# Threshold attention and an ELU feed-forward on one core: head pairs 5 to 9 take the two-step structure, and the first stage is ordered from a list of jobs with needs

## The chip, the cores and the metric

The kernel runs on one core of one Trainium2 chip. The metric is the device time of one execution in microseconds (us), and lower is better. The engines are named as the profile names them: PE (matrix products, with PEld for its weight loads), DVE (vector engine), ACT (activation engine), POOL (GpSimd) and SP, from whose queue nearly all transfers are issued. Each engine executes its own instructions in the order in which the program lists them; semaphores join the engines.

## The reference

There are 8 sequences of 576 tokens with 8 heads of 64 channels, all fp32. Attention keeps only the scores that lie within `tau` of the row's maximum; its output, 4608 tokens by 512 channels, goes through two matrix products with an ELU between them (512 to 2048 to 512).

```python
def _attn_ref(q, k, v, tau):
    scale = 1.0 / np.sqrt(q.shape[-1])
    scores = scale * np.matmul(q, k.transpose(0, 1, 3, 2))
    thresh = np.max(scores, axis=-1, keepdims=True) - tau
    scores = np.where(scores >= thresh, scores, -1000000000.0)
    scores = scores - np.max(scores, axis=-1, keepdims=True)
    attn = np.exp(scores)
    attn = attn / (np.sum(attn, axis=-1, keepdims=True) + 1e-09)
    return np.matmul(attn, v).astype(np.float32)

def _moe_ref(x, w_in, w_out):
    h = x @ w_in
    g = np.where(h > 0.0, h, np.exp(np.minimum(h, 0.0)) - 1.0)
    return (g @ w_out).astype(np.float32)
```

## The kernel before

**Pairs and steps.** Two heads form a pair, four pairs a sequence, so there are 32 pairs, numbered 0 to 31 in the code (pairs 5 to 9 of the title are 4 to 8 there, and the code's numbers are used from here on). A pair has five steps: four row blocks of 128 query tokens (both heads, 576 scores per row and head) and one step for the last 64 tokens of both heads together (`NC`). A step goes through these operations: scores on PE (`scores`), the row maximum on DVE (`max_of`), the bound on POOL (`bound_of`), the exponential on ACT (`exp_of`), the mask with its row sum on DVE (`mask_of`), the sum of the two head sums and a reciprocal on DVE (`total_of`, `reciprocal_of`), and the normalization on POOL (`normalize`). Then the weights must be transposed. Either PE does it in three or two parts through a PSUM bank and ACT copies the result (`turn_parts`), or DVE turns 32x32 squares and four stores to DRAM and one load put the squares in place (`turn_squares`, `fetch`). Last come the products with `v` (`values`, `values_out`).

**The two-step structure.** Pairs 9 to 31 run in a loop at the end of the kernel that holds one set of five PSUM banks (`wide`) for all scores. A pair has a short tail step, in which its 64-token scores share PE with the values of the pair before the last (`tails_and_values`), and two halves, each of which writes the scores of two row blocks and two heads at once into the five banks (`wide_scores`). The next writing of a bank waits for the masks that read it. The weights live in just two buffers (`turned_by`), and all steps are turned in squares. After each half, 14 quarters of the feed-forward (`first_product`, `second_round`, a Strassen-like scheme with seven products in place of eight, 0.86 us each) are put on PE. The loop's order comes from `on_pe`, `at` and a table of written shifts, `MOVED`.

**The first stage.** Everything ahead of that loop is made by `early_tasks`: all of pairs 0 to 8 in the one-step structure (score buffers of two banks per head, three weight buffers), the first sequence's feed-forward in 64 plain halves (`ffn1`, `ffn2_plain`, 8 or 4 products each), the conversion of the 32 pieces of `w_in` and `w_out` from their raw words (`convert_rest`, `convert_shift`, `convert_add`, `convert_abs`, `convert_end` on ACT, DVE, POOL, ACT and DVE), and the sums of weight blocks that the loop's scheme needs (`make_in`, `change_in`, `make_out`). `task` gives each of these a written time, from a base of 5.0 us a step for ten steps and 7.2 us a step after that, shifted by `MOVED`; the program is listed in the order of these times, each task's needs ahead of it. In the first ten steps `spare` puts transposes of the identity on PE, 132 with those at the start. At the change from the first stage's pools to the loop's, `leave_early` closes one pool and opens another in its place.

**What decides the order of other queues.** SP's queue takes loads, stores of turned squares and fetches in the same listing; an entry that waits for a semaphore holds up what is behind it.

## Time and profile before

| | us |
|---|---|
| three runs, median (lowest to highest) | 1306.32 (1305.8 to 1308.91) |
| span of the profiled execution, first to last instruction | 1304.1 |
| span to median of the runs | 2.2 |
| first stage: start to the first tail step of pair 9 | 284.7 |
| of that, DVE busy | 231.1 |
| one pair of the loop, from pair 11's tail step to pair 12's | 34.1 |

The page of the profile has a row of busy tenths for each engine in 40 slices of 32.6 us, and the trace can be asked for busy times of stretches, for groups of equal instructions, for waits and for the instructions in order of time. PE matmuls are pipelined: their durations overlap, so what one costs is read from the distance between starts. A PE that counts as busy can still have gaps within a group.

### The profile page before, as it was taken

How to read it: one execution, taken by the hardware profiler on the slowest of the kernel's cores; microseconds unless marked ns; L12 is line 12 of the kernel's file. 1: busy time of each engine (PE TensorE's matmuls, PEld its weight loads, DVE VectorE, ACT ScalarE, POOL GpSimd, SP SyncE). 2: the span in 40 equal slices, each digit the busy share in tenths (PEclk: the TensorE clock that was granted, in tenths of full speed). 3: DMA queues.
4: the chain of work that ended last, by engine and by line, in shares of the span. 5: the costliest groups of instructions: out<-in, count | busy, mean ns of one | idle time of the engine just before them, and what ended most of it. 6: DMA issues, size and time to landing. Idle time of an engine off the chain costs nothing.

```text
span 1304.1 us, 21747 instructions
## 1 busy us (share of the span) xinstructions
PE 1278.2 (98%) x6822; PEld 994.8 (76%) x6822; DVE 1022.4 (78%) x2218; ACT 552.0 (42%) x1196; POOL 800.6 (61%) x1190
## 2 busy tenths in 40 slices
PE   9999999889999999999999999999999999999998
PEld 7675566346888887878878878878787888888887
DVE  6888887789888988898889889897989882545534
ACT  5777633225252535344444444353525260421320
POOL 4678645878466765766576747574858473524533
PEclk9999999899999999999999999999999999999999
DMA  7546377788888999899889888989899875222211
GB/s 148 125 149 175 99 208 201 224 212 259 216 242 238 260 229 254 224 253 232 226 221 263 236 238 219 257 242 246 221 260 252 228 217 171 85 73 68 86 61 33
DMA packets 327828, 256.02 MB, mean 196 GB/s; under 512 B 209312, under 2 KB 288672, under 8 KB 327712
## 3 DMA queue, kind: packets, MB, share of 16 engines
q1 hardware_dynamic: 325776, 254.14, 71.0%
q8 instruction: 54, 0.88, 0.3%
q10 hardware_dynamic: 1936, 0.48, 0.2%
q14 instruction: 62, 0.51, 0.1%
HBM read 165.94 MB, written 88.60 MB: 195 GB/s over the span
## 4 chain that ended last, share of the span: by engine, by line
PE 85%; DVE 5%; POOL 3%; issue 2%; DMA 1%; ACT 1%; SPq 1%; DVEq 0%; POOLq 0%; ACTq 0%
PE f L1441 30%; PE f L1301 28%; PE sc L663 7%; PE sc L723 7%; PE f L774 3%; PE sc L393 3%; PE rt L471 2%; PE f L814 2%; PE pv L616 1%; POOL w L427 1%; DVE w L454 1%; PE sc L715 1%; PE sc L710 1%; DVE mx L431 1%; DMA there<-x 1%
## 5 line engine op out<-in xcount | busy, mean ns | idle before, releaser
L427 POOL TENSOR_SCALAR w<-w,rs 128x576 f32<-128x576 f32 x196 | 163.1, 841 | 88.5 <-DVE rs L468 85.7
L670 DVE TENSOR_REDUCE mx<-sc 128x1 f32<-128x576 f32 x207 | 148.2, 749 | 29.7 <-PE sc L663 25.8
L680 ACT ACTIVATE w<-sc,mx 128x576 f32<-128x576 f32 x115 | 82.9, 740 | 118.3 <-DVE mx L670 96.4
L1301 PE MATMUL f<-xt,sw 128*128 128x256 f32 x512 | 124.2, 385 | 1.0 <-ACT xt L733 0.5
L1301 PE MATMUL f<-xt,w_in_sb 128*128 128x256 f32 x512 | 122.2, 381 | 0.1
L550 DVE STREAM_TRANSPOSE x<-w 128x512 f32<-128x512 f32 (+2 forms) x163 | 107.2, 692 | 13.9 <-POOL w L427 13.6
L676 POOL TENSOR_SCALAR th<-mx,ntau 128x2 f32<-128x2 f32 (+1 forms) x115 | 34.3, 299 | 136.1 <-DVE mx L670 136.1
L1301 PEld LDWEIGHTS f<-xt,sw 128*128 128x128 f32 x512 | 93.7, 190 | 21.3 <-issue 5.2
L1301 PEld LDWEIGHTS f<-xt,w_in_sb 128*128 128x128 f32 x512 | 96.2, 190 | 15.9 <-ACT w L1315 2.7
L1301 PE MATMUL f<-x,w_in_sb 128*128 128x256 f32 x448 | 106.1, 379 | 1.4 <-ACT g L1362 1.4
L1441 PE MATMUL f<-w_out_sb,g 128*128 128x256 f32 x448 | 107.1, 382 | 0.0
L1441 PE MATMUL f<-w_out_sb,s 128*128 128x256 f32 x448 | 107.0, 382 | 0.0
L1441 PE MATMUL f<-t,s 128*128 128x256 f32 x448 | 105.8, 379 | 0.0
L663 PE MATMUL sc<-kT,qT 64*128 64x448 f32 (+4 forms) x736 | 103.2, 416 | 1.4 <-DVE w L684 1.4
L663 PEld LDWEIGHTS sc<-kT,qT 64*128 64x128 f32 x736 | 80.6, 186 | 26.4 <-issue 16.8
L1388 POOL TENSOR_TENSOR s<-g 128x256 f32<-128x256 f32 x104 | 80.4, 778 | 29.4 <-PE f L1441 20.1
L684 DVE SCALAR_TENSOR_TENSOR w<-sc,th,w 128x576 f32<-128x576 f32 x115 | 89.7, 810 | 10.3 <-ACT w L680 10.1
L1301 PEld LDWEIGHTS f<-x,w_in_sb 128*128 128x128 f32 x448 | 85.0, 190 | 13.3 <-ACT g L1362 1.8
L1441 PEld LDWEIGHTS f<-w_out_sb,g 128*128 128x128 f32 x448 | 84.1, 190 | 14.2 <-issue 3.2
L1441 PEld LDWEIGHTS f<-w_out_sb,s 128*128 128x128 f32 x448 | 84.2, 190 | 13.5 <-issue 2.5
L1441 PEld LDWEIGHTS f<-t,s 128*128 128x128 f32 x448 | 85.1, 190 | 11.6
L427 POOL TENSOR_SCALAR e<-e,rs 128x576 f32<-128x576 f32 x92 | 68.5, 748 | 35.3 <-DVE rs L468 33.8
(204 smaller groups left out, 2813.1 us busy)
## 6 DMA issues: line engine op xcount, KB each, us to landing
there<-x SPq DMA_DIRECT2D x436, 144.0 KB, 3.4
wTb<-there SPq DMA_DIRECT2D x56, 576.0 KB, 6.5
wTa<-there SPq DMA_DIRECT2D x53, 576.0 KB, 4.9
sw<-win_sums SPq DMA_DIRECT2D x62, 384.0 KB, 4.2
t<-wout_sums SPq DMA_DIRECT2D x45, 512.0 KB, 5.5
qm<-in_q_dram SPq DMA_DIRECT2D x124, 72.0 KB, 4.7
vm<-in_v_dram SPq DMA_DIRECT2D x64, 128.0 KB, 3.1
wst<-in_moe_w_in_dram SPq DMA_DIRECT2D x16, 512.0 KB, 4.6
```

The costliest lines, as they stand in the source:

```text
L393: nc.tensor.matmul(scs[h][:, a, :HALF], qs[r], kT[r, k0 : k0 + HALF], start=True, stop=True)
L427: nc.gpsimd.tensor_scalar(wv, wv, st["rs"][:, h : h + 1], 1.0, ALU.mult, ALU.mult)
L550: nc.vector.transpose(x[:, :, c0 : c0 + nc_], src.rearrange("p (c g n) -> p g c n", c=nc_, n=T))
L663: on_banks(nc.tensor.matmul(o, qT[r, i * P : (i + 1) * P], kT[r, k0 : k0 + n], start=True, stop=True, skip_group_check=True), o)
L670: on_banks(nc.vector.tensor_reduce(st["mx"][:, h : h + 1], st["sc", h], axis=AX.XY if i == NC else AX.X, op=ALU.max, negate=True), st["sc" ...
L680: on_banks(nc.scalar.activation(st["e", h], st["sc", h], AF.Exp, bias=st["mx"][:, h : h + 1]), st["sc", h])
L684: on_banks(nc.vector.scalar_tensor_tensor(st["e", h], st["sc", h], st["th"][:, h : h + 1], st["e", h], ALU.is_ge, ALU.mult, accum_out=st[" ...
L723: on_banks(nc.tensor.matmul(o, vm[:, h, c], parts[part][:, g0:g1, h * (NC + 1) + c], start=False, stop=(c == NC - 1), skip_group_check=Tru ...
L774: nc.tensor.matmul(loc["ph"][:, k], w_in_sb[:, j, ft * P : (ft + 1) * P], xts[g][:, j, hf * CT : (hf + 1) * CT], start=(j == 0), stop=(j = ...
L1301: nc.tensor.matmul(loc["banks"][place], left[:, j], right[:, j], start=(begins and j == 0), stop=(j == 1), skip_group_check=True)
L1388: engine.tensor_tensor(o, x, y, op)
L1441: nc.tensor.matmul(place(m), lhs, rhs, start=(begins and v == 0), stop=(v == RU - 1), skip_group_check=True)
```

## The change

Pairs 4 to 8 leave the one-step structure: `JOINED` (the first pair in two steps) goes from 9 to 4, while the loop still starts with pair 9, now called `START`. The whole of the first stage is expressed as jobs: each has an engine, a written cost, a written due time, the jobs that it needs, and the PSUM banks that it uses. `schedule` keeps one clock per engine and repeatedly lists the job that can start first by those clocks; on an engine, jobs that can start within a small allowance of the earliest are taken by due time. The numbers of the due times stand in a table `PR` in place of most of `MOVED`; the entries of `MOVED` for the loop stay as they were.

With it come these edits:

- The five banks of `wide` exist from the start. Pairs 0 to 3 use four of them as two score buffers, the fifth and three further banks are lent out by `schedule` for transposes, values and feed-forward.
- The order of pairs 0 to 3 is all first row blocks, all second ones, then the rest pair by pair; the values of the first two row blocks are formed one block at a time (`values(..., block=...)`), and half of the first sequence's `ffn1` works on 128 tokens at a time (`ffn1_block`).
- One weight buffer and the two square buffers get pools that last for the whole kernel; two weight buffers serve pairs 4 to 8, as in the loop.
- 32 of the first stage's normalizations and 14 of its sums go to ACT (`normalize_act`, `total_act`), 10 `convert_rest` and 16 of 24 `make_in` go to POOL.
- Steps of pairs 4 to 8 are turned in squares except two of pair 4; of pairs 0 to 3 one step is turned in squares.
- Transposes of the identity are put on PE only in gaps before 24 us of the scheduler's clock (`PR["warm"]`), 127 in all.
- The values of pair 7 move into the tail step of pair 9, and the input sums of the second sequence (`sums_x`) into the loop's pair 9.

```diff
+PR = {'wait_pe': 0.262,
+ 'wait_dve': 0.141,
+ 'wait_act': 0.187,
...
+ 'b0': 6.944,
+ 'p0': 4.249,
+ 'p1': 6.0,
+ 'p2': 24.241,
...
+ 'warm': 24.083,
+ 'part_b': [[4, 0], [4, 2], [5, 1], [5, 2], [6, 3]],
+ 'squares': [12]}
...
+    def convert_rest_pool(i):
+        if i in staged:
+            lo = staged[i][:, :, 0]
+            nc.gpsimd.tensor_scalar(lo.bitcast(FP32), lo, 2.0**-51, 2.0, ALU.mult, ALU.add)
...
+    turned_by = w_one, e_both.rearrange("p e a n -> p (e a n)")
...
-        if "f" in psum and not apart:
-            both = psum["s"].tile([P, 2, 2, 512], FP32, name="sc")
-            scs = {h: both[:, h] for h in hs}
-        else:
-            scs = {h: psum["s"].tile([P, 2, 512], FP32, name="sc") for h in hs}
+        for h in hs:
+            scs[h] = slots[slot_no[0] % 2]
+            slot_no[0] += 1
...
+    def normalize_act(pr, i, h):
+        st = open_steps[pr, i]
+        wv = st["w"][:, h * S : (h + 1) * S]
+        nc.scalar.mul(wv, wv, st["rs"][:, h : h + 1])
+
+    def total_act(pr, i, hs):
+        st = open_steps[pr, i]
+        cs = slice(hs[0], hs[-1] + 1)
+        st["summed"] = True
+        nc.scalar.activation(st["su"][:, cs], st["sm"][:, cs, 0], AF.Identity, bias=st["sm"][:, 0, 1:2])
...
-            for _ in range(spare.pop() if spare else 0):
-                transpose(rt[:, 0], ident)
...
+    def ffn1_block(i, x):
+
+        loc = {}
+
+        def part(k):
+            if k == 0:
+                loc["ph"] = bank()
+            for a in range(2 * k, 2 * k + 2):
+                ft = 4 * x + a
+                for j in range(KJ):
+                    nc.tensor.matmul(loc["ph"][:, a * P : (a + 1) * P], w_in_sb[:, j, ft * P : (ft + 1) * P],
+                                     xts[0][:, j, i * P : (i + 1) * P], start=(j == 0), stop=(j == KJ - 1))
...
-    JOINED = (2 * NPAIR + 1)
+    JOINED = NPAIR
...
-    steps[:per_seq] = [(pr, i) for x in ((0, 1), (2, 3, NC)) for pr in range(NPAIR) for i in x]
+    steps[:per_seq] = [(pr, i) for x in ((0,), (1,), (2, 3, NC)) for pr in range(NPAIR) for i in x]
...
+    START = 2 * NPAIR + 1
...
+        def schedule():
...
+            while left:
+                best = None
+                for e, mine in open_.items():
+                    starts = []
+                    for r, x in mine:
+                        t = room(x) if jobs[x][5] or jobs[x][11] or jobs[x][12] else when[x]
+                        if t is not None:
+                            starts.append((max(t, free[e]), r, x))
+                    if starts:
+                        limit = min(starts)[0] + PR.get("wait_" + e, 0.0)
+                        t, r, x = next(y for y in starts if y[0] <= limit)
+                        if best is None or t < best[0]:
+                            best = t, e, r, x
...
+                if e == "pe" and gap > 0.7 and t < PR["warm"] and idents:
+                    got = [b for b in banks_of if free_at(b, "pe") is not None and free_at(b, "pe") <= free["pe"] + 0.3]
+                    if got:
+                        count = int((gap - 0.5) / 0.112)
...
+                job(("tail", pr), "pe", 1.25, t + ob["tail"], lambda pr=pr, v=v, loc=loc: loc.update(zip(("main", "outs"), tails_and_values(pr, v))),
...
+                job(("wsc", pr, half), "pe", 2.2, t + ob["wsc"], lambda pr=pr, half=half: wide_scores(pr, half), ("tail", pr) if not half else ("wsc", pr, 0),
+                    ("prep", "q", pr), ("prep", "k", pr), *wide_users, form="s", wide_banks=(0, 1, 2, 3, 4))
...
-        for pr in range(JOINED, NP + 2):
+        for pr in range(START, NP + 2):
...
-                if b > 2:
+                if b > 1:
                     xs = [late["x"].tile([P, 2, CT], FP32, name=f"x{x}") for x in range(3)]
                     jobs = sums_x(b - 1, xs)
...
-            begin = 4 if pr == JOINED else 0
-            ffn_quarters(begin)
             for half in range(2):
                 if pr < NP:
                     wide_step(pr, half)
-                ffn_quarters(HALF_QUARTERS - (0 if half else begin))
+                ffn_quarters(HALF_QUARTERS)
```

## The prediction

> **What bounds the kernel now.** I read the page's rows by slices first, then busy times by stage, then the waits, then single steps in order of time. The slices show one long stage with PE always busy, so the question is where PE only seems busy.
>
> ```profile
> span 1304.1 us, 21747 instructions
> PE   9999999889999999999999999999999999999998
> PEld 7675566346888887878878878878787888888887
> DVE  6888887789888988898889889897989882545534
> ```
>
> PE's row says 9 everywhere. Its weight-load row says something else: 3 to 7 in slices 1 to 9, some 8 after that. So the first 285 us hold fewer products per us than the loop. Stretches show the same (columns: length, busy us and instructions of PE, PEld, DVE, ACT, POOL, granted clock, DMA share, GB/s):
>
> ```profile
> 0.00:20.00 20.00, 17.77 (x113) 14.93 (x114) 12.38 (x30) 7.99 (x14) 7.57 (x28) 1.00 0.67 121
> 20.00:122.00 102.00, 98.16 (x591) 69.79 (x590) 86.50 (x186) 78.23 (x160) 74.92 (x106) 1.00 0.54 152
> 122.00:284.70 162.70, 152.37 (x681) 87.08 (x679) 132.26 (x300) 66.36 (x132) 104.43 (x159) 0.98 0.70 190
> 353.50:387.60 34.10, 34.10 (x193) 27.27 (x192) 28.58 (x65) 19.12 (x44) 20.44 (x32) 1.00 0.88 245
> ```
>
> The loop's pair (last line) loads weights 80% of the time; 122 to 284.7, where pairs 4 to 8 run in the old structure, only 54%. DVE is at 81% there, so neither engine is full. The waits of PE in the first 330 us confirm that it waits for chains through DVE and POOL:
>
> ```profile
> PE sc L393 <- DVE w L454: 7.1, 6, 5.3
> PE rt L471 <- POOL w L427: 4.8, 9, 0.8
> ```
>
> The one wait of 5.3 us lies at 243, where a step waits for the mask ahead of it while pools are exchanged:
>
> ```profile
> 242.08 1.24 PE L393 MATMUL sc<-kT,qT 64*128 64x288 f32 x8
> 248.65 2.26 PE L393 MATMUL sc<-kT,qd 128*128 128x288 f32 x4 [5.33 <-DVE w L454]
> ```
>
> The granted clock falls with it: 0.98 over that stage, half speed for some 7 us. The loop from 284.7 on takes 1304.1 - 284.7 = **1019.4 us**, PE-bound, and its code hardly changes. So the change is worth what it takes off 284.7. I count to the first tail step of pair 9 in both programs, with counts from the listing of instructions.
>
> **PE.** From starts in order of time: a two-head score step of the old form 1.17 us, a tail one 0.97, a transpose 0.109, values 2.44 (two blocks) and 3.04 (three), a feed-forward half 1.73; of the loop, tail with values 1.13, values 4.03, a half's scores 2.14.
>
> ```profile
> 353.54 0.45 PE L710 MATMUL sc<-kT,qT 64*64 64x288 f32 x1
> 354.67 2.37 PE L723 MATMUL sc<-wTb,vm 128*64 128x320 f32 x16
> 356.87 1.90 PE L723 MATMUL sc<-wTa,vm 128*64 128x256 f32 x16
> 358.70 2.21 PE L663 MATMUL sc<-kT,qT 64*128 64x448 f32 x16
> 360.84 1.99 PE L1301 MATMUL f<-xt,sw 128*128 128x256 f32 x8
> 373.12 2.21 PE L663 MATMUL sc<-kT,qT 64*128 64x448 f32 x16
> 387.63 0.45 PE L710 MATMUL sc<-kT,qT 64*64 64x288 f32 x1
> ```
>
> Before: 36 x 1.17 + 9 x 0.97 = 50.9 scores, 132 idle and 234 real transposes 39.9, values 9 x 2.44 + 8 x 3.04 = 46.3, 64 halves 110.7: **248**. After: 16 x 1.17 + 4 x 0.97 = 22.6, 127 + 177 transposes 33.1, eight block values, 4 x 3.04, 64 halves, five tails, three of them with values, ten halves of scores: 5 x 1.13 + 3 x 4.03 + 21.4 = 39.1. A block value is not in the trace: half of 2.44 from below, 2.44 from above; its columns halve, so 1.22, in all 9.8 for the 9.8 removed. The 128-token `ffn1_block` is 16 products of 128 columns in place of 8 of 256: 1.73 if each takes half of 0.216, up to 16 x 0.19 = 3.0 if weight loads (mean 190 ns) set it. Transposes load new weights every 109 ns, the nearest row, so 1.73; the other end would be +21 us of PE work where PE still waits for weights to be converted. Sum after: 227, **21 us less**.
>
> **DVE.** 231.1 busy us before; the sum of its durations is 259, as neighbours overlap, so 0.89 a us. Masks and maxima stay at 81 each. Removed: 16 `make_in` x 0.495, 15 sums x 0.156, two input sums: 11.6. Added: turns. Before 32 x 0.687 + 14 x 0.278 + 4 x 0.20 = 26.7; after 23 x 0.687, 16 x 0.84 (row of the loop), 11 x 0.27: 32.2. Net -6, so **225 busy us**. DVE's work does not shrink; all turns on how densely it is packed.
>
> **ACT and POOL.** ACT, 152.6 busy us of 284.7, gains 32 normalizations (bounded by a 512-column conversion, 0.69, and a 576-column exponential, 0.742: 24), 14 sums (0.16 to 0.28: 3), and loses 10 conversions (7) and a fifth of its transposed copies (8). About 165. POOL, 186.9, loses 34 normalizations x 0.863 and 20 bounds x 0.296 (35) and gains 16 x 0.73 + 10 x 0.64 (18): 168. Neither binds at 250; what is moved onto ACT stands in front of exponentials in its queue, and the masks behind those on DVE wait; `make_in` on POOL stands in front of bounds in the same way. I price that inside the pace of a pair below.
>
> **Transfers and SP.** Turns rise from 59 to 83 stores and fetches from 14 to 23. SP takes some 0.5 us an entry (four stores 1.76 to 2.58 us), 40 entries a pair, 20 us: hidden under a pair of 26, but each store waits for its turn with loads behind it. In the loop the DMA share is 0.88 of 34.1 us, 30 us a pair; without the weight sums, 1.5 of 8.3 MB in the largest packets, I take 25. Five pairs at 25 and some 20 for converted weights and sums, less what is not yet due (pair 8's fetches, two steps turned on PE: 20) make 125 us of full DMA.
>
> **Opening stretch.** Pairs 0 to 3: 36 heads x (0.746 + 0.811 + 0.082), 28 shifts x 0.692, 27 ends x 0.707, sums, preparation, eight others: 120 us of DVE, 107 busy. 12.4 are done by 20 us as before. The other 94 at 92% (DVE's row shows 9 in many slices) take 102: pair 4 starts at **121**. At 81%, today's share, 136; taking over today's exact 123.8 costs 3 more. From below 117.
>
> **Pairs 4 to 8.** In the loop, a half holds the five banks from its first score to its last mask for 9.8 to 10.8 us (median 10.77), a tail step for 3.8 to 5.4. One example:
>
> ```profile
> 360.62 2.09 DVE L670 TENSOR_REDUCE mx<-sc 128x1 f32<-128x576 f32 x3 [0.88 <-PE sc L663]
> 364.85 0.82 DVE L684 SCALAR_TENSOR_TENSOR e<-sc,th,e 128x576 f32<-128x576 f32 x1 [1.04 <-ACT e L680]
> 368.66 0.81 DVE L684 SCALAR_TENSOR_TENSOR w<-sc,th,w 128x576 f32<-128x576 f32 x1
> 372.14 1.42 DVE L550 STREAM_TRANSPOSE x<-w 128x640 f32<-128x640 f32 x2
> ```
>
> Scores at 358.70, last mask done at 369.5. There 12.3 us of products hide it; with only some 7 us of feed-forward a half left, the banks set the pace: 2 x 10.3 + 4.6 = 25.2 us a pair, 23.3 from the shortest. The two weight buffers set another: the buffer that masks leave at 369.5 is normalized and turned by 373.6, 14.9 us after the scores; the next tail's exponential (2.1 us after its start) needs it. Tail to half 5.2, half to half 10.3, half to tail 12.8: 28.3. The loop has no hurry with that turn, so I stay nearest to the banks: **26 us, 130 for five**. PE's own 120 us and DVE's 118 lie under it.
>
> So the loop starts at 121 + 130 = 251. It then costs 1019.4, plus 4.0 (pair 7's values, now in pair 9) and 0.9 (pair 8's in the shared form), less today's stall in pair 9: 34.8 us without its values where 34.1 - 4.0 would do, 4.7; I take half as gone: 1022. Span 1273; the runs' median lies 2.2 above the span: **1275 us**.
>
> **A rule against it.** The change drops fillers after 24 us. The trace has one gap of PE over 3.4 us after its start, at 243, and after it the clock was halved for 6.8 us, so 3.4 us of work lost. After 24 us the opening still has some 80 us of PE work in 97, so I count no new gap. The Trainium skill (TensorE: Matmul & The Clock Gate, "What's actually happening") says that one idle window of about 3.4 us is enough for half speed, which agrees with that gap. If by this rule two new gaps fell into the opening, the sum would be 1282 in place of 1275.
>
> **Rivals.** (1) DVE packed as loosely as today in the opening and weight buffers at 28.3: 131 + 141.5 = 272.5, loop 1022: **1297**. For: 81% over the whole stage. Against: those waits come from one written order with pool changes. (2) Transfers set the second part: 125 us at the loop's 0.88 share is 142, start at 263: **1287**. For: no stretch of the first stage today is above 0.86. Against: a fetch has a whole pair's time. (3) Slower: the ring of two weight buffers and ACT. The place is the pair's pace. If added normalizations and PSUM copies delay each exponential so that a pair takes over 34 us, 121 + 5 x 34.6 = 294, the end is at 294 + 1022 + 2 = **1318**; it decides from 33.8 us a pair at 121. Today's old form takes 32.2 a pair, so the new one must be slower than that. Against: 28.3 counts each hand-over at leisure. (4) The list only reshuffles: pairs still at 32.2, start at 282, loop 1022: **1306**, no change.
>
> **How the numbers follow.** Likeliest case, pair at 23.3 to 28 and opening 117 to 127: 0.64, own range 1258 to 1292. Rivals 1 and 2 together 0.18, below 1258 0.03, rival 4 0.03, rival 3 0.12. 0.3% (3.9 us) is about what can be told from no change here. Faster 0.85, same 0.03, slower 0.12. The range, 1256 to 1303, leaves out some 2 in 100 below and rivals 3 and 4 above.
>
> **What would show it.** In the new profile: the first product of the loop (now line 1487) at about 256, the first wide scores near 124, weight-load tenths of 6 to 7 in slices 4 to 7 in place of 3 to 6, DVE's 9 there, a period of 26 us between tails of pairs 4 to 8, waits of PE for DVE masks under 2 us each, and a loop pair still at 34.1. Wrong if tails are over 30 us apart, if waits for fetched tiles appear, or if loop pairs lengthen.

## The result: 1.5% slower, and the profile after

The changed kernel takes **1326.76 us** (median of four runs, 1325.55 to 1329.91) where the kernel before takes 1307.62 (four runs, 1305.8 to 1309.47): a ratio of 1.0148, 95% interval 1.0128 to 1.0168. 1275 was predicted, with a range of 1256 to 1303, so the prediction is wrong by 52 us and in its sign. The profiled execution has a span of 1324.6 us.

First the rows of the changed kernel's page in 40 slices of 33.1 us (busy tenths of PE, PE's weight loads and DVE, and the granted clock in tenths):

```profile
span 1324.6 us, 22023 instructions
...
PE   7889988998999999999999999999999999999998
PEld 6667546546788878787878787878788887888887
DVE  4788779779888997989798979898889882545534
...
PEclk9789999999999999999999999999999999999999
```

Counted from 0, slices 4 to 7 have weight loads at 5, 4, 6 and 5, where 6 to 7 was foreseen, and DVE at 7, 7, 9 and 7, where 9 was. PE shows gaps (7, 8) in five of the first seven slices, where it had 9 throughout before, and the clock is at 7 to 9 tenths in slices 0 to 2. The same by stretches (length, busy us and instructions of PE, PEld, DVE, ACT and POOL, granted clock, DMA share, GB/s). The bounds are the first tail step of pair 4 (152.8) and that of pair 9 (302.5); the last line is one pair of the loop:

```profile
20.00:122.00 102.00, 88.93 (x605) 67.37 (x606) 80.00 (x165) 73.20 (x150) 67.13 (x89) 0.88 0.58 149
...
152.80:302.50 149.70, 133.70 (x588) 77.63 (x587) 119.62 (x255) 64.75 (x119) 79.77 (x118) 0.97 0.78 210
0.00:302.50 302.50, 267.15 (x1497) 180.13 (x1497) 229.01 (x483) 164.93 (x323) 172.15 (x252) 0.94 0.69 178
340.80:374.80 34.00, 34.00 (x195) 27.49 (x194) 29.42 (x65) 10.67 (x22) 21.23 (x33) 1.00 0.88 226
```

Pair 4 starts at 152.8 (predicted 121, before 123.8), the five pairs take 149.7 us, 29.9 each (predicted 26, before 32.2), and pair 9 starts at 302.5 (predicted 251, before 284.7). From there on it is 1324.6 - 302.5 = 1022.1 us, where 1022 was predicted. So the whole miss lies ahead of the loop: 32 us in the opening, 20 us in pairs 4 to 8. The engines have the work that was foreseen (DVE 229.0 busy us, ACT 164.9, POOL 172.2; predicted 225, 165, 168). What failed is how densely it is packed: from 20 us to pair 4's start DVE is busy 102.4 of 132.8 us, 77%, where 92% was taken.

The waits of pairs 4 to 8 say who waits for whom (engine, line and tile, releaser: us in all, times, longest):

```profile
PE sc L703 <- DVE w_one L677: 12.9, 5, 2.9
...
DVE x L534 <- DMA there<-x: 8.7, 3, 3.7
...
DVE mx L663 <- PE sc L656: 5.3, 3, 2.8
...
DVE w_one L677 <- POOL th L669: 2.9, 1, 2.9
```

PE's tail steps wait 12.9 us in five waits for the masks ahead of them, 2.9 at most (under 2 was foreseen). DVE in its turn waits for stores of turned squares, for scores, and for a bound that POOL owes it. None of these is large; they follow one another on one chain. The first wide scores came at 157.6 us (124 was foreseen), the loop's first product at 311.9 (256).

### The profile page after: what moved, and what is told of

It is laid out like the page before. It is cut to its first block, busy times and chain, and to the rows that moved or that the text cites. A ratio compares the mean times of both kernels' runs of the same rounds, so it can differ in the third digit from the quotient of the medians.

```text
span 1324.6 us, 22023 instructions
## 1 busy us (share of the span) xinstructions
PE 1282.4 (97%) x7000; PEld 1007.8 (76%) x7000; DVE 1023.9 (77%) x2190; ACT 567.0 (43%) x1221; POOL 788.5 (60%) x1152
## 4 chain that ended last, share of the span: by engine, by line
PE 77%; DVE 8%; POOL 5%; DMA 3%; issue 3%; ACT 2%; SPq 1%; DVEq 0%; POOLq 0%; ACTq 0%
PE f L1627 29%; PE f L1487 27%; PE sc L716 8%; PE sc L656 7%; DVE mx L663 2%; PE sc L708 1%; PE sc L394 1%; DMA there<-x 1%; POOL wtop L256 1%; PE sc L703 1%; POOL t L951 1%; DVE x L534 1%; DVE mx L418 1%; DVE e L677 1%; PE f L460 1%
## 5 line engine op out<-in xcount | busy, mean ns | idle before, releaser
L663 DVE TENSOR_REDUCE mx<-sc 128x1 f32<-128x576 f32 x252 | 179.2, 748 | 33.8 <-PE sc L656 29.5
L673 ACT ACTIVATE w_one<-sc,mx 128x576 f32<-128x576 f32 x140 | 101.2, 740 | 133.4 <-DVE mx L663 110.5
L669 POOL TENSOR_SCALAR th<-mx,ntau 128x2 f32<-128x2 f32 (+1 forms) x140 | 42.8, 306 | 182.6 <-DVE mx L663 182.5
L402 POOL TENSOR_SCALAR w_one<-w_one,rs 128x576 f32<-128x576 f32 x137 | 112.3, 830 | 52.4 <-DVE rs L457 52.1
L656 PE MATMUL sc<-kT,qT 64*128 64x256 f32 (+5 forms) x896 | 126.2, 416 | 1.6 <-DVE w_one L677 1.6
L656 PEld LDWEIGHTS sc<-kT,qT 64*128 64x128 f32 x896 | 98.6, 186 | 34.5 <-issue 20.8
L677 DVE SCALAR_TENSOR_TENSOR w_one<-sc,th,w_one 128x576 f32<-128x576 f32 x140 | 109.6, 810 | 14.8 <-ACT w_one L673 11.4
L534 DVE STREAM_TRANSPOSE x<-w_one 128x512 f32<-128x512 f32 (+1 forms) x140 | 99.9, 743 | 24.5 <-POOL w_one L402 15.2
L673 ACT ACTIVATE e<-sc,mx 128x576 f32<-128x576 f32 x112 | 82.0, 744 | 56.7 <-DVE mx L663 54.8
L677 DVE SCALAR_TENSOR_TENSOR e<-sc,th,e 128x576 f32<-128x576 f32 x112 | 87.9, 809 | 9.9 <-ACT e L673 8.8
```

Source lines behind the costliest of these rows:

```text
L402: nc.gpsimd.tensor_scalar(wv, wv, st["rs"][:, h : h + 1], 1.0, ALU.mult, ALU.mult)
L534: nc.vector.transpose(x[:, :, c0 : c0 + nc_], src.rearrange("p (c g n) -> p g c n", c=nc_, n=T))
L656: on_banks(nc.tensor.matmul(o, qT[r, i * P : (i + 1) * P], kT[r, k0 : k0 + n], start=True, stop=True, skip_group_check=True), o)
L663: on_banks(nc.vector.tensor_reduce(st["mx"][:, h : h + 1], st["sc", h], axis=AX.XY if i == NC else AX.X, op=ALU.max, negate=True), st["sc" ...
L669: nc.gpsimd.tensor_scalar(st["th"][:, cs], st["mx"][:, cs], -1.0, ntau, ALU.mult, ALU.add)
L673: on_banks(nc.scalar.activation(st["e", h], st["sc", h], AF.Exp, bias=st["mx"][:, h : h + 1]), st["sc", h])
```

## The experiments

Each run below names what it gives for three places: the start of pair 4, the start of pair 9, and the median of the run. The medians of the kernel before beside them were 1305.6 to 1307.6, so runs can be compared to about 2 us. The start of pair 4 is less steady: five kernels that list the opening as the changed kernel does (xo, tailfill, x3, identq and x3b) put it at 149.4 to 154.6, so what is read from it alone holds to some 3 us.

| kernel | pair 4 | pair 9 | median | ratio to before, 95% |
|---|---|---|---|---|
| changed | 152.8 | 302.5 | 1326.8 | 1.0148 (1.0128 to 1.0168) |
| order | 139.6 | 301.2 | 1327.6 | 1.0161 (1.0144 to 1.0178) |
| rest | 146.5 | 296.9 | 1321.0 | 1.0104 (1.0089 to 1.0119) |
| acts | 148.2 | 310.6 | 1334.7 | 1.0211 (1.0195 to 1.0226) |
| warm | 150.9 | 300.8 | 1325.6 | 1.0140 (1.0125 to 1.0155) |
| xo | 152.2 | 300.0 | 1324.4 | 1.0144 (1.0129 to 1.0160) |
| tailfill | 153.2 | 304.8 | 1328.8 | 1.0179 (1.0163 to 1.0195) |
| ordrest | 142.1 | 304.3 | 1325.7 | 1.0148 (1.0132 to 1.0165) |
| all4 | 141.4 | 324.2 | 1341.7 | 1.0287 (1.0259 to 1.0314) |
| x3 | 154.6 | 298.9 | 1327.4 | 1.0158 (1.0143 to 1.0173) |
| identq | 149.4 | 300.8 | 1326.7 | 1.0149 (1.0133 to 1.0164) |
| hand | 141.3 | 300.4 | 1322.4 | 1.0120 (1.0105 to 1.0135) |
| ordhid | 130.6 | 296.3 | 1320.1 | 1.0104 (1.0083 to 1.0125) |
| ohx | 129.6 | 289.2 | 1312.3 | 1.0049 (1.0030 to 1.0069) |
| x3b | 149.6 | 299.2 | 1323.1 | 1.0131 (1.0110 to 1.0153) |
| best1 | 129.4 | 289.7 | 1310.9 | 1.0039 (1.0024 to 1.0054) |
| ohxc | 131.0 | 284.2 | 1310.3 | 1.0030 (1.0020 to 1.0040) |
| best4 | 130.8 | 279.6 | 1302.5 | 0.9971 (0.9959 to 0.9983) |
| noorder | 138.4 | 292.1 | 1315.7 | 1.0073 (1.0056 to 1.0090) |

### Four suspects of the opening

**order**: the first steps in the old order.

```diff
-    steps[:per_seq] = [(pr, i) for x in ((0,), (1,), (2, 3, NC)) for pr in range(NPAIR) for i in x]
+    steps[:per_seq] = [(pr, i) for x in ((0, 1), (2, 3, NC)) for pr in range(NPAIR) for i in x]
```

> The order of the first steps is that of before again ((0, 1) of each of the first four pairs, then (2, 3, tail)); all else is as changed. In the changed kernel the first score steps start at 9.14, 20.67, 30.85, 38.0, 43.0, 49.1 us, before at 7.29, 10.36, 16.0, 21.6, 26.4, 31.0, and pair 4 starts at 152.8 (before 123.8). Theory T1 (the new order asks for four pairs' loads in the first four steps, and the loads set the opening): the second step starts by 13, the fourth by 26, pair 4 at 130 to 140, the whole run 13 to 20 us shorter than the changed kernel. Theory T2 (clock halved by gaps, whatever the order): the steps still lie apart, half-speed stretches remain between 24 and 80 us, and less than 6 us is gained. Theory T3 (normalizations and sums moved to ACT stand ahead of exponentials): less than 4 us gained, since they stay. Pairs 4 to 8 keep 29.9 us a pair by all three.

The score steps start at 8.5, 13.0, 20.3, 26.6, 32.6 us, nearly as T1 said, and pair 4 at 139.6, within T1's 130 to 140. But the run takes 1327.6, where T1 had 13 to 20 us less than the changed kernel. Pair 4 lasts 40.8 us in place of 31.8, and by pair 9 the 13 us are gone. T1 is right on the opening and wrong on what it is worth. What became of the gain is answered further on, under ordrest.

**rest**: the turn of the rest of pair 0's q is listed ahead of the first two maxima.

```diff
-        job("rest", "dve", 0.55, beg(0) + off["rest"], rest_of_q, ("prep", "q", 0), begin=8.9)
+        job("rest", "dve", 0.55, -96.5, rest_of_q, ("prep", "q", 0), begin=7.1)
```

> Only rest_of_q is listed ahead of the first two maxima on DVE, as before the change, so that the load of pair 1's q, which waits for its buffer until 12.3 us, may start some 3 us earlier. T1: the second and all later steps of the opening start about 3 us earlier, pair 4 at 149 to 150, the run 2 to 4 us shorter than the changed kernel. T2 and T3: the start of the second step moves, but pair 4 stays at 152 to 153 and the time within 1 us.

In the changed kernel SP's queue waits for that turn (L1136) before it can load pair 1's q. DVE does it at 11.75 to 12.4, behind the maxima; SP's queue (first line DVE, second SP; start, length, operation, idle time before):

```profile
11.75 0.57 DVE L1135 STREAM_TRANSPOSE x<-qm 128x384 f32<-128x384 f32 x1
12.24 0.20 DVE L1136 STREAM_TRANSPOSE qe<-qm 128x64 f32<-128x64 f32 x1
```

```profile
7.56 0.51 SPq L314 DMA_DIRECT2D vf<-in_v_dram  x1
12.47 3.05 SPq L298 DMA_DIRECT2D qm<-in_q_dram  x4
```

SP issues nothing from 8.1 to 12.47, with the loads of pair 1 next in its queue and those of pairs 2 and 3 behind them. With the edit the turn is done at 8.1, pair 4 starts 6.3 us earlier and the run is 5.8 us shorter: more than T1's 2 to 4, and here nearly all of it is kept. The last weight is converted 5.2 us earlier too (170.4 in place of 175.6), so what waits for the weights moves along.

**acts**: normalizations and sums that went to ACT are back on POOL and DVE.

```diff
-        su_act = {tuple(x) for x in PR["su_act"] if not isinstance(x, int)}
-        act_norm, in_pool = set(map(tuple, PR["act_norm"])), set(map(tuple, PR["in_pool"]))
+        su_act = set()
+        act_norm, in_pool = set(), set(map(tuple, PR["in_pool"]))
...
-            if n in PR["su_act"]:
+            if False:
```

> Normalizations and sums of the first stage that the change put on ACT are on POOL and DVE again; the order of steps and the two-step structure stay. T3: exponentials come earlier, pair 4 starts at 140 or before, pairs 4 to 8 take 28 us or less, the run is 10 us or more shorter than the changed kernel. T1 and T2: pair 4 stays at 150 to 156; POOL has 24 us more work and DVE 3 us more, so that the run is between 2 us shorter and 6 us longer.

8 us longer, so T3 falls: moving them to ACT was a gain of 8 us. POOL is busy for 195.8 us ahead of pair 9 in place of 172.2, and pair 5 takes 44.4 us in place of 27.2 (pair 4 25.9 in place of 31.8). That was the first sign that POOL, not ACT, owes something in pairs 4 to 6.

**warm**: fillers in all gaps that the list plans.

```diff
- 'warm': 24.083,
+ 'warm': 400.0,
```

> The limit of 24 us for filler transposes is lifted: wherever the list plans PE idle for over 0.7 us, transposes of the identity fill it. That adds 41 of them, all in the part of the list that runs between 24 and 75 us, none ahead of the tails of pairs 4 to 9. T2: fewer half-speed stretches before 80 us (37 us of them lay at 29.6 to 77 with gaps and work in the changed kernel, four stretches of 23.8 us in sum), so up to 8 us of PE work regained and pair 4 at 145 to 150. T1: the loads set the opening, so filling the gaps gives less than 2 us, though the clock rises.

Half speed before 80 us falls from 23.9 us (four stretches) to 13.7 (two), and the run is 1.2 us shorter, inside the scatter. So 10 us less of half clock in the opening made no difference that can be told. The 41 fillers are work for PE themselves, and the 13.7 us that remain were not tested.

### Pairs 4 to 8: sums on POOL, the clock, or the stores

**xo**: the sums of weights get an earliest time each in the list.

```diff
-            job(("xo", k), "pool", 1.26, begin_b(0) + PR["xo0"] + PR["xo1"] * k, lambda: extra.popleft()[2](), "late", ("xo", k - 1) if k else None)
+            job(("xo", k), "pool", 1.26, begin_b(0) + PR["xo0"] + PR["xo1"] * k, lambda: extra.popleft()[2](), "late", ("xo", k - 1) if k else None, begin=170 + 7.0 * k)
...
-                    ("in", u, x - 1) if x else ("in", u - 1, 2) if u else None, "late", ("insend", u - 2) if u > 1 and not x else None)
+                    ("in", u, x - 1) if x else ("in", u - 1, 2) if u else None, "late", ("insend", u - 2) if u > 1 and not x else None,
+                    begin=172 + 3.0 * (3 * u + x))
```

> The sums of feed-forward weights on POOL (t L951, 12 of 1.24 us) and on POOL and DVE (sw L923) get an earliest time each, 7 and 3 us apart, so that they spread over pairs 5 to 8; in the changed kernel all 28 on POOL run in one stretch from 176 to 218 us, among the bounds (th L669) and normalizations that the masks and turns of pairs 4 and 5 wait for. Theory T5 (these sums hold the bounds): the second half of pair 4 holds its banks 10 to 12 us in place of 18.5, the first tail step of pair 9 comes at 290 to 296 (302.5), the run is 6 to 12 us shorter than the changed kernel. Theory T4 (stores of turned squares hold DVE in pairs 4 to 8): the sums only change places, 302.5 stays within 3 us and so does the time. The opening stays as it is by both (pair 4 at 152.8).

Half of each theory came true. The second half of pair 4 holds its banks for 14.0 us (18.5), pairs 4, 5 and 6 take 28.6, 23.0 and 29.1 in place of 31.8, 27.2 and 31.2: 9.5 us gained. Pairs 7 and 8, beside which the sums now run, take 33.7 and 33.4 in place of 30.6 and 28.9: 7.6 lost. Whether the sums cost the same there is not shown, because more than the sums has moved: pair 8 now has 12 halves of feed-forward where it had 8, seven of them in one piece of 12.2 us, and from 203 to 300 the second products of the feed-forward are the largest share of the chain (21.9%). In these later pairs the chain of xo also runs through stores of squares of 5.7 and 5.9 us.

**tailfill**: products with the identity ahead of the tail steps, in columns that no score uses.

```diff
+                if x[0] == "tail" and x[1] > NPAIR:
+                    o = wide[0][:, : 2 * T]
+                    for _ in range(20):
+                        on_banks(nc.tensor.matmul(o, idents[-1], idents[-1][:, : 2 * T], start=True, stop=True, skip_group_check=True), o)
                 run(x, t)
```

> Ahead of the tail steps of pairs 5 to 8 PE gets 20 products of 64 columns with the identity into columns that no score uses; they wait only for the first mask of the half before, not for the last, so PE works in the 2 to 3 us in which it waits for the other masks. All else is in the same order. Theory T2 (the wait halves the granted clock, and each half-speed stretch of 3.4 us costs on the path): no half-speed stretch at the tails of pairs 6, 7 and 8 (214, 244.7, 275.4 us), tail with values 5.2 us in place of 8.0, pair 9's first tail step at 294 to 297, the run 5 to 8 us shorter. Theory T4 (the chain through DVE and the stores sets the pace, PE has slack): the stretches are gone but the tails stay 29 to 31 us apart, less than 2 us gained.

Here are 8 us from the first tail step of pairs 6, 7 and 8, in the changed kernel and then in this one; the clock is the third number from the end:

```profile
211.80:219.80 8.00, 7.82 (x49) 4.10 (x50) 6.88 (x15) 3.06 (x8) 7.05 (x11) 0.79 0.66 166
243.00:251.00 8.00, 7.91 (x49) 3.90 (x50) 7.49 (x17) 3.60 (x9) 2.79 (x7) 0.79 0.74 188
273.60:281.60 8.00, 7.91 (x49) 4.04 (x50) 7.26 (x16) 3.52 (x8) 1.25 (x3) 0.79 0.93 216
```

```profile
215.60:223.60 8.00, 8.00 (x64) 5.07 (x64) 6.59 (x14) 2.57 (x6) 4.26 (x7) 1.00 0.78 170
246.30:254.30 8.00, 8.00 (x64) 5.12 (x65) 6.74 (x15) 2.57 (x6) 3.90 (x7) 1.00 0.82 185
276.20:284.20 8.00, 8.00 (x60) 4.37 (x61) 5.62 (x13) 2.57 (x6) 0.51 (x2) 1.00 0.87 198
```

The clock is whole again and the values behind the tails take 4.03 us in place of 5.3 to 5.7. Yet pair 9 comes 2.3 us later. Pairs 6 to 8 take 30.6, 29.9 and 28.6 us, 1.6 us less in sum than in the changed kernel; the loss lies ahead of them, in pairs 4 and 5 (34.4 and 28.1 in place of 31.8 and 27.2). The experiment is not as clean as its expectation: each product runs as two passes, so the 20 took 4.5 to 4.6 us, more than the 2.4 to 2.9 us of waiting that they replaced, and most of what the clock gave the fillers took. What it does show is the size: the halved clock costs 1.3 to 1.7 us a tail, some 4.5 us in these three pairs, of the 20 that are missing.

**ordrest** and **all4**: combinations of the above (ordrest: order and rest; all4: these with xo and tailfill). The new lines of ordrest, then those that all4 adds:

```diff
+    steps[:per_seq] = [(pr, i) for x in ((0, 1), (2, 3, NC)) for pr in range(NPAIR) for i in x]
+        job("rest", "dve", 0.55, -96.5, rest_of_q, ("prep", "q", 0), begin=7.1)
```

```diff
+                    begin=172 + 3.0 * (3 * u + x))
+                if x[0] == "tail" and x[1] > NPAIR:
+                    o = wide[0][:, : 2 * T]
...
```

> Old order of the first steps and rest_of_q ahead of the first maxima together. If the two causes in the opening add: pair 4 starts at 131 to 135 (139.6 with the order alone, 146.5 with rest_of_q alone, 152.8 as changed). If pairs 4 to 8 go by the moment at which all weights are converted and the sums made (the last conversion ended at 170.6 with the order alone, 175.6 as changed), pair 9 starts at 294 to 298 and the run takes 1314 to 1320; if they keep 30 us a pair, pair 9 starts at 283 and the run takes 1305.

> Old order of the first steps, rest_of_q first, spread sums and filler products ahead of tails, all four together. If the four causes are separate and each gives what its theory says, pair 9 starts at 274 to 284 and the run takes 1297 to 1306, at or under the time of before. If stores and loads set the pace of pairs 5 to 8, these still take 29 to 30 us each, pair 9 starts at 286 to 292 and the run takes 1308 to 1314.

Neither adds up. ordrest starts pair 4 at 142.1, so with the old order the place of that turn of q no longer matters, and pair 4 then takes 40.7 us, as with order alone. In all4 the fillers are hit by the low clock themselves (40 passes in 8.6 us ahead of pair 7) and stand in front of tails that have already lost time; 324.2 at pair 9, in an execution that took 1348.8, 7 us above the median. Adding gains of single edits is no forecast while it is not known what gives them back.

The trace of order shows where its gain went. Pair 4 loses 9.0 of the 13.2 us, but PE waits only 2.8 us in it: it does 17 halves of feed-forward there where the changed kernel has 12. In pair 5 it then has 2 left in place of 8, nothing hides a wait any more, and PE is busy 16.7 of 30.9 us. What it waits for shows a few us into pair 5. First DVE, then POOL (start, length, operation, and in brackets the idle time before it and what ended it):

```profile
182.36 0.41 DVE L923 TENSOR_TENSOR sw<-w_in_sb 128x256 f32<-128x256 f32 x1
191.17 0.82 DVE L677 SCALAR_TENSOR_TENSOR w_one<-sc,th,w_one 128x576 f32<-128x576 f32 x1 [8.40 <-POOL th L669]
```

```profile
185.05 1.26 POOL L951 TENSOR_TENSOR t<-w_out_sb 128x512 f32<-128x512 f32 x1 [2.78 <-DMA wout_sums<-t]
186.28 1.47 POOL L402 TENSOR_SCALAR e<-e,rs 128x576 f32<-128x576 f32 x2
187.72 1.26 POOL L951 TENSOR_TENSOR t<-t,w_out_sb 128x512 f32<-128x512 f32 x1
188.94 0.72 POOL L923 TENSOR_TENSOR sw<-w_in_sb 128x256 f32<-128x256 f32 x1
189.62 1.26 POOL L951 TENSOR_TENSOR t<-w_out_sb,t 128x512 f32<-128x512 f32 x1
190.87 0.27 POOL L669 TENSOR_SCALAR th<-mx,ntau 128x1 f32<-128x1 f32 x1
```

DVE is idle for 8.4 us because the mask of the tail step needs the bound `th` of 190.87. That bound is 0.27 us of work and its maximum was ready at 182.4, but four sums and two normalizations stand ahead of it on POOL, and the first of the sums waited 2.78 us for a store that empties its room. POOL is only 57% busy ahead of pair 9, yet DVE, and behind it PE, wait for it.

### Hand-overs

**x3**: a third buffer for turned squares, in room that the loop's sums use later.

```diff
-        x = squares.tile([P, NT, NCH, T], FP32, name="x")
+        turned_no[0] += 1
+        if late and pr < START and turned_no[0] % 3 == 0:
+            x = late["x"].tile([P, 6 * CT], FP32, name="xall")[:, : NT * NCH * T].rearrange("p (g c n) -> p g c n", c=NCH, n=T)
+        else:
+            x = squares.tile([P, NT, NCH, T], FP32, name="x")
...
-                    turns_b[-2] if len(turns_b) > 1 else None, ("sc", number[1, NC]))
+                    turns_b[-3] if len(turns_b) > 2 else None, ("sc", number[1, NC]), "late")
```

> Turned squares of pairs 4 to 8 get a third buffer (in the room that three sums of the loop use later), so that DVE's turn (x L534) no longer waits for the stores of the turn two before it. In the changed kernel DVE waits there 8.7 us in three waits in pairs 4 to 8, and the chain of these pairs runs through stores of 5 to 7.6 us. Theory T4 (these stores set the pace): the waits of DVE x L534 for the store are gone, pairs 6 to 8 take 27 to 28 us each in place of 30.2, pair 9's first tail step comes at 294 to 297 (302.5), the run is 5 to 8 us shorter than the changed kernel. Rival (weight conversions and their sums on POOL set it): 302.5 within 2 us.

Pairs 6, 7 and 8 take 27.2, 27.7 and 25.0 (31.2, 30.6, 28.9): 10.8 us, more than T4 said, and the turn's wait for a store is no longer among the costliest of that stretch. But pair 4 takes 5 us more, since all its turns now wait for the new room, and pair 9 takes 46.2 in place of 38.3, with this wait in it:

```profile
DVE xall L976 <- DMA there<-xall: 7.1, 1, 7.1
```

The room is shared with sums of the loop (L976), which now wait for the last store out of it.

**identq**: the identity for the turns of pair 4 by PE is made early, in a tile of the first four pairs.

```diff
-            idents.append(late["x"].tile([P, RU, P], FP32, name="s3", bufs=1)[:, 0])
-            make_identity(nc, idents[-1])
...
+        def new_ident():
+            make_identity(nc, qds[0])
+            idents.append(qds[0])
+
+        job("ident", "pool", 0.6, begin_b(0) - 20.0, new_ident, ("sc", number[2, NC]))
```

> The identity for the five steps of pairs 4 to 6 that PE turns is made in a tile that the first four pairs have done with, so it is there before pair 4; in the changed kernel it is made when the staging room of the weights closes, after the last weight conversion (170 us), and the first of these turns follows at 170 to 172, after which the second half of pair 4 gets its weight buffer. The order of all engines' work is the same. Theory T6 (pair 4 waits for that identity): its second half holds its banks 11 to 14 us in place of 18.5, pair 5 starts at 178 to 181 in place of 184.7, the run 2 to 5 us shorter. Rival (PE would have come to that turn no earlier, because feed-forward products ahead of it wait for the same last weights): less than 1 us gained.

No effect: the second half still holds its banks for 18.1 us, pair 4 takes 32.3, the run 1326.7. T6 falls. (The expectation speaks of five turns by PE; there are two, both in pair 4.)

**hand**: the PSUM bank in which the first stage's transposes and values land, and which is one of the five of the new structure, is left alone from the last three steps of pair 3 on.

```diff
-            return b != "t" or x[0] in ("put", "out") or x == "idle0"
+            return b != "t" or x[0] == "put" and x[1] < 17 or x[0] == "out" and x[1] < 3 or x == "idle0"
...
-        job("t", "none", 0.0, begin_b(0) - 20.0, leave_t, *[("~", "put", m, x) for m in range(per_seq) if m not in SQUARES for x in range(2 + (steps[m][1] < NC))],
-            *[("~", "out", pr, 1) for pr in range(NPAIR)])
+        job("t", "none", 0.0, begin_b(0) - 20.0, leave_t, *[("~", "put", m, x) for m in range(17) if m not in SQUARES for x in range(2 + (steps[m][1] < NC))],
+            *[("~", "out", pr, 1) for pr in range(3)])
```

> The PSUM bank in which transposes and values of the first stage land and which is one of the five banks of the second structure is left free from the last three steps of pair 3 on (they use the three other banks). In the changed kernel pair 4's first tail step waits until these are done: it comes 16.8 us after the last score step of pair 3 (136.0 to 152.8), where in the kernel before the next pair's scores came 6.3 us after. Theory T7 (this hand-over is a term of its own, about 10 us): pair 4 starts at 140 to 145, all later pairs move with it, pair 9 starts at 291 to 296. Rival (what follows goes by the last weight conversion and the sums behind it): pair 4 starts earlier, but pair 5 stays at 180 or later and pair 9 at 299 or later, the time within 3 us of the changed kernel.

PE in the changed kernel between pair 3's last scores and pair 4's first:

```profile
135.41 2.28 PE L394 MATMUL sc<-kT,qd 128*128 128x288 f32 x4 [2.36 <-DVE w L443]
...
145.92 0.38 PE L460 MATMUL sc<-ident,w 128*64 128x128 f32 x2
...
147.86 0.81 PE L601 MATMUL f<-wTb,vd 128*128 128x384 f32 x2
148.60 2.37 PE L606 MATMUL f<-wTb,vm 128*64 128x320 f32 x16
...
152.82 1.19 PE L703 MATMUL sc<-kT,qT 64*64 64x288 f32 x8
```

and with the edit:

```profile
135.53 1.24 PE L394 MATMUL sc<-kT,qd 128*128 128x288 f32 x4 [1.99 <-DVE w L443]
...
140.67 0.66 PE L460 MATMUL f<-ident,w 128*128 128x128 f32 x4 [0.38 <-ACT wTb L481]
141.26 0.94 PE L703 MATMUL sc<-kT,qT 64*64 64x288 f32 x6
```

In the changed kernel the last transposes, the values of pair 3 and a feed-forward half come first, 17.4 us from score to score; with the edit 5.7. Pair 4 starts 11.5 us earlier, as T7 said. But pair 5, from 174.5 on, takes 37.4 in place of 27.2, and the run is 4.4 us shorter. Pair 9 is where the rival put it (300.4, 299 or later), the time a little better than its 3 us; pair 5 comes earlier than its 180.

**ordhid**: order, hand and identq together.

```diff
+    steps[:per_seq] = [(pr, i) for x in ((0, 1), (2, 3, NC)) for pr in range(NPAIR) for i in x]
+            return b != "t" or x[0] == "put" and x[1] < 17 or x[0] == "out" and x[1] < 3 or x == "idle0"
+        job("ident", "pool", 0.6, begin_b(0) - 20.0, new_ident, ("sc", number[2, NC]))
```

> Old order of the first steps, the bank of the last transposes free early and the identity made early, together. If the three are the terms of the late opening: pair 4 starts at 126 to 131, pair 5 at 156 to 164, pair 9 at 280 to 288 and the run takes 1302 to 1310. If a gain at pair 4 is given back in pairs 4 to 8 as with the old order alone: pair 9 at 296 or later, 1320 or more.

Pair 4 at 130.6, pair 5 at 162.0, both as foreseen; then pair 5 takes 42.6 us and pair 9 starts at 296.3. The chain from 160 to 206 by engine and line:

```profile
by line: POOL t L951 24.9%; issue 13.0%; DMA wst<-in_moe_w_out_dram 11.5%; DVE mx L663 11.5%; DVE e L677 7.0%; POOL sw L923 6.7%; DVE x L534 6.3%; SPq L568 3.5%; PE sc L703 2.7%; POOL e L402 1.9%; DVE sw L923 1.9%; DVE w_one L677 1.6%; POOL
```

A quarter of it is `t L951`, the sums on POOL. They can only start when the last weight is converted, and that is at nearly the same time whenever pair 4 starts: 175.6 as changed, 170.6 in order, 178.9 in hand, 174.6 here. The earlier pairs 4 and 5 start, the further into them these sums fall. That is where the gains of hand and ordhid went: in hand, too, `t L951` is the largest share (31.9%) of pair 5's chain.

### Taking the causes away together

**ohx**: order, hand and xo. **x3b**: x3 for pairs 4 to 7 only, without the wait for its room. **best1**: order, hand, xo and x3b. First the new lines of ohx, then x3b against x3; best1 has both:

```diff
+    steps[:per_seq] = [(pr, i) for x in ((0, 1), (2, 3, NC)) for pr in range(NPAIR) for i in x]
+            return b != "t" or x[0] == "put" and x[1] < 17 or x[0] == "out" and x[1] < 3 or x == "idle0"
+                    begin=172 + 3.0 * (3 * u + x))
```

```diff
-        if late and pr < START and turned_no[0] % 3 == 0:
+        if late and pr < START - 1 and turned_no[0] % 3 == 0:
...
-                    turns_b[-3] if len(turns_b) > 2 else None, ("sc", number[1, NC]), "late")
+                    turns_b[-3] if len(turns_b) > 2 else None, ("sc", number[1, NC]))
```

> Old order of the first steps, the bank of the last transposes free early, and the sums of weights with an earliest time each (as alone before): the sums come 7 and 3 us apart over pairs 6 to 8 in place of one stretch from 175 to 212 us. With the old order, the early bank and the early identity pair 4 started at 130.6 and pair 5 at 162.0, and then pair 5 took 42.6 us, with the sums on POOL (t L951) as 25% of its chain. Theory T5 (the gain at pair 4 is lost to these sums): pair 5 takes 25 to 29 us, pair 6 starts at 184 to 192 (204.5), pair 9 at 277 to 285, the run takes 1300 to 1308. Rival (the sums cost the same wherever they run before the loop): pair 6 starts early but pairs 6 to 8 take 34 us and more, pair 9 at 290 or later, 1314 or more.

> The third buffer for turned squares again, but only in pairs 4 to 7 and without a wait for its room ahead of the turns of pair 4. With it pairs 6 to 8 took 27.2, 27.7 and 25.0 us (31.2, 30.6, 28.9 in the changed kernel), while pair 4 took 5 us more and pair 9 7.9 us more, the latter with DVE waiting 7.1 us for stores out of the shared room (xall L976). Theory T4 (two buffers and their stores set pairs 6 to 8, and the two losses came from how the third was made): pair 4 and 5 as changed (31.8 and 27.2), pairs 6 and 7 at 27 to 28, pair 9 starts at 293 to 298 and takes 38.3, the run takes 1316 to 1321. Rival (what the third buffer gives is lost again at the next wait): 1324 or more.

> Old order, early bank, spread sums and third buffer together. If the terms are separate (opening 22 us, sums 10 us, stores 6 us): pair 4 at 128 to 131, pairs 4 to 8 at 27 us, pair 9 at 264 to 272, the run takes 1288 to 1296, under the time of before. If one wait takes the place of the other: pair 9 at 280 or later, 1304 or more.

ohx confirms T5 for the place in question: pair 5 takes 25.7 us where ordhid's took 42.6, pair 6 starts at 186.8, and the run falls to 1312.3. But pairs 7 and 8 take 32.9 and 39.1, so that pair 9 (289.2) and the run lie between T5 and its rival. x3b gains 3.7 us, not the 5 to 11 expected: pair 6 takes 26.1, but pair 7 37.8, since its list puts 28 feed-forward products, 12.2 us in one piece, ahead of pair 8's tail. best1 has pairs 5, 6 and 7 at 26.5, 26.1 and 30.5 and then loses it in pair 8, 45.8 us. There POOL does this between two bounds:

```profile
277.23 0.27 POOL L675 TENSOR_SCALAR th<-mx,ntau 128x2 f32<-128x2 f32 x1 [8.82 <-DVE mx L669]
277.45 10.98 POOL L937 TENSOR_TENSOR w_in_sb<-w_in_sb 128x256 f32<-128x256 f32 x16
288.40 0.29 POOL L675 TENSOR_SCALAR th<-mx,ntau 128x2 f32<-128x2 f32 x1
```

and PE:

```profile
268.05 12.28 PE L843 MATMUL f<-w_out_sb,g 128*128 128x512 f32 x28
289.70 0.71 PE L709 MATMUL sc<-kT,qT 64*64 64x288 f32 x1 [9.37 <-DVE w_one L683]
```

16 subtractions (`change_one`) in one piece, 10.98 us, stand ahead of a bound of 0.29 us; PE finishes seven halves of feed-forward at 280.3 and waits 9.37 us for the mask behind that bound.

**ohxc**: ohx with the subtractions behind that bound. **best4**: best1 with the same, and the third buffer up to the first half of pair 8.

```diff
-                job(("chg", u, x), "pool", 0.72, begin_b(0) + PR["ch0"] + PR["ch1"] * (2 * u + x), lambda u=(u + 2) % NU, x=x: change_one(u, x), *last1, ("in", NU - 1, 2), ("insend", NU - 1))
+                job(("chg", u, x), "pool", 0.72, begin_b(0) + PR["ch0"] + PR["ch1"] * (2 * u + x), lambda u=(u + 2) % NU, x=x: change_one(u, x), *last1, ("in", NU - 1, 2), ("insend", NU - 1), ("bth", START - 1, 3))
...
-        if late and pr < START - 1 and turned_no[0] % 3 == 0:
+        if late and (pr < START - 1 or pr < START and i != 2 and i != 3) and turned_no[0] % 3 == 0:
```

> As ohx (old order, early bank, spread sums; two buffers for squares), with the 16 subtractions behind the last bound of pair 8. ohx took 1312.3, pair 8 39.1 us, pairs 6 and 7 30.4 and 32.9. T5: pair 8 takes 29 to 33 us, pair 9 starts at 279 to 284, the run takes 1302 to 1307. T4 (stores with two buffers) says that it stays 2 to 6 us over the same kernel with three buffers (best4); if stores do not matter, the two are within 1 us.

> As best1 (old order, early bank, spread sums, third buffer), with the third buffer also in the tail and first half of pair 8, and the 16 subtractions on POOL (w_in_sb L937, 10.98 us in one piece) listed behind the last bound of pair 8; in best1 they stood ahead of it, DVE's last masks and pair 9's first tail step waited for them (277.5 to 288.7 us of the chain), and pair 8 took 45.8 us. Theory T5 (work for the weight sums on POOL ahead of bounds): pair 8 takes 33 to 37 us, of which 12 are seven halves of feed-forward that PE has left, pair 9 starts at 277 to 281, the run takes 1298 to 1302, 0.4 to 0.6% under the time of before. Rival (PE, half its clock and the left halves, would be no earlier): pair 9 at 286 or later, 1307 or more.

best4 takes **1302.5 us**, a ratio of 0.9971 (0.9959 to 0.9983) to the kernel before: 0.3% less than that, with an interval that stays under 1, and 24 us less than the changed kernel. Pair 8 takes 36.2, pair 9 starts at 279.6. Its rows and its stretches (opening, pairs 4 to 8):

```profile
span 1300.7 us, 21979 instructions
...
PE   8899899899999999999999999999999999999998
...
PEclk9899999999999999999999999999999999999999
```

```profile
20.00:130.80 110.80, 98.84 (x726) 75.54 (x726) 89.69 (x191) 84.21 (x175) 75.41 (x103) 0.95 0.62 157
130.80:279.60 148.80, 140.48 (x639) 82.31 (x638) 125.07 (x272) 72.03 (x135) 88.38 (x123) 0.99 0.85 230
```

PE is busy 140.5 of 148.8 us there (133.7 of 149.7 as changed), and the clock is nearly whole without a filler there: with most of the waits, most of the halving has gone too. Yet the five pairs take 148.8 us, hardly less than the 149.7 of the changed kernel: the whole gain at pair 9 is the earlier start of pair 4. Pairs 5 and 6 take 25.3 and 26.1, but pair 8 has 12 halves of feed-forward where the changed kernel has 8, and seven of them stand in one piece of 12.2 us ahead of pair 9. No run took these halves out of pair 8. ohxc differs only by having two buffers for squares and takes 1310.3, so the third buffer is worth 7.8 us here, more than T4's 2 to 6; 4.6 of them show at the start of pair 9 and 3.0 within pair 9. In the kernels ahead of these it was worth less: 3.7 from the changed kernel to x3b, 1.4 from ohx to best1. In ohxc DVE waits this long for stores from pair 4 to 8:

```profile
DVE x L534 <- DMA there<-x: 13.2, 4, 6.4
```

In best4 the turns have no such wait among the costliest of that stretch. ohxc itself misses its 1302 to 1307: pair 8 takes 34.1 (39.1), 5 us as said, but pair 9 takes 40.6 (38.0), with the subtractions as 12% of its chain, so 2 us remain of 5.

**noorder**: best4 with the changed kernel's order of the first steps.

```diff
-    steps[:per_seq] = [(pr, i) for x in ((0, 1), (2, 3, NC)) for pr in range(NPAIR) for i in x]
+    steps[:per_seq] = [(pr, i) for x in ((0,), (1,), (2, 3, NC)) for pr in range(NPAIR) for i in x]
```

> As best4 (early bank, spread sums with the subtractions behind the last bound, third buffer), but with the changed kernel's order of the first steps (step 0 of four pairs, then step 1 of four pairs). On the changed kernel the old order started pair 4 13 us earlier and won nothing in the end. Theory T1 with T5 (the order's cost was real, and hidden only because the sums on POOL and the stores gave it back): pair 4 starts at 140 to 144 (130.8 in best4), pair 9 at 288 to 294 (279.6), the run takes 1310 to 1317. Rival (what follows takes up the difference here too, for instance because PE's feed-forward work sets the end): pair 4 late, pair 9 at 283 or earlier, 1306 or less.

1315.7, 13.2 us more than best4, with pair 4 at 138.4 and pair 9 at 292.1: T1 with T5. Taken back alone on the changed kernel, the same edit was worth nothing. The start of pair 4 moved less than foreseen (7.6 us in place of 9 to 13); the rest came in pair 8, where PE had eight halves of feed-forward left (14.0 us in one piece) and took 42.2 us.

## Why the prediction was wrong, step by step

**"Pair 4 starts at 121": it failed, 152.8.** The step took DVE's work and a density of 92%. DVE did about the foreseen work, 109.4 busy us for 107, but only 7.0 of it by 20 us, where the step has 12.4 "as before", and the rest at 77%. The density was put in by choice; what sets it was not costed. (The step's own terms, 20 + 102, give 122.) Two terms are shown by runs. The order of the first steps needs four pairs' loads in the first four steps: 13.2 us at pair 4 in order, 7.6 in noorder against best4; while that order stands, 6.3 for the turn that SP's loads wait for (rest; with the old order it no longer counts, as ordrest shows). The hand-over through the shared bank: 11.5 us (hand). The working of the step named neither. It went over how many instructions each queue has, and not in which order they stand, though the listing shows the turn behind the maxima and the loads behind one another. With both causes gone pair 4 starts at 129.4 to 131.0; the 8 to 10 us that are left to 121 (6 to 7 to the 123.8 of before) were not followed up.

**"26 us a pair": it failed, 29.9, and for five pairs no run reached it.** Single pairs took 25 to 26.5 us (pairs 5 and 6 in best4 25.3 and 26.1, in best1 26.5 and 26.1), so the bank chain of 25.2 was read well, and the weight-buffer ring of 28.3 was not the limit. What the step left out lies beside the pairs. The first missing term is POOL's order: "what is moved onto ACT stands in front of exponentials ...; `make_in` on POOL stands in front of bounds in the same way. I price that inside the pace of a pair". That price was at most the 0.8 us between 25.2 and 26, and the waits behind 28 sums and 16 subtractions, all after the last converted weight, cost more. The best measure for the sums is ordhid to ohx, 7.8 us of run, although two edits differ there (identq, which alone did nothing, is the other); for the subtractions ohx to ohxc, 2.0. The second is the stores of turned squares out of two buffers, 7.8 us between ohxc and best4; rival 2 had transfers in mind, but as a share of bandwidth, and it is the wait for a buffer that costs. These terms do not make up the 20 us: best4 is free of most of them, and its five pairs still take 29.8 us on average, with pair 4 at 32.0 and pair 8 at 36.2.

**"I count no new gap": wrong in fact, small in cost.** Half speed came in nine stretches before 307 us, 41 us in sum, and each gap of PE ahead of a tail from pair 6 on was followed by one. The waits there were 2.81 us (ending at 211.83) and 2.92 us (ending at 243.00), and half speed began 2.1 and 1.7 us after their ends. The rule that was set against the change, the Trainium skill's (TensorE: Matmul & The Clock Gate, "What's actually happening"), speaks of one idle window of about 3.4 us; here waits shorter than that were enough, while the wait of 2.2 us ahead of pair 5's tail was not. The price of 3.4 us for the gap at 243 in the kernel before was too high as well: the half clock there ran from 245.8 to 252.6 and the wait ended at 248.65, so only 4.0 us of it fell on work, 2.0 us lost. Two new gaps were priced at 7 us by it. The runs put the tails of pairs 6 to 8 at some 4.5 us in sum, and warm shows nothing clear of the scatter in the opening.

**The rivals.** The third had the sign right, and a wrong mechanism: ACT. acts shows that ACT's share was a gain of 8 us. Its numbers (a pair over 33.8 us) did not occur either; the end came late by a late start. The first (loose DVE, 131 + 141.5) comes nearest in kind, with 272.5 for 302.5. (Two of their numbers do not follow from the working: today's share of 81% gives 136 there and not 131, and with 121 for the start the 0.3% that is called slower is reached from 33.0 us a pair.)

**What was right.** The work of DVE, ACT and POOL to 3% (POOL's terms add up to 170, not 168), and the bank chain as the pace of an undisturbed pair. The loop was right to 0.1 us (1022.1 for 1022), but that closely by luck: pair 9 took 38.3 us where the terms give 37.4, and the loop pairs behind it took 34.0 in place of 34.1.

Still open: the 8 to 10 us of the opening named above, what pair 8 would take without the feed-forward that is left to it, and why pair 4 itself takes 31 to 32 us even in best4 (32.0) and its relatives. The trace of best4 points at the weights: loads of the raw words of `w_out` are 30.5% of the chain of its pair 4, and steps of their conversion (`wtop`, `w_out_sb`) another 20%. No run takes these away. In sum, best4 has regained 24 of the 52 us; of the rest some 10 lie ahead of pair 4 (130.8 for 121) and 19 in pairs 4 to 8 (148.8 for 130).
